# A windowed attention and highway kernel: four half-wide stages for the first pair of batches, other routes for V and for x, and one PSUM ring

## The chip, the cores and the metric

The kernel runs on one NeuronCore of a Trainium2 chip. The metric is device time in microseconds (us) of one execution; less is better. A core has a matrix engine (PE), a vector engine (DVE), an activation engine (ACT), a general engine (POOL) and a queue engine (SP). PE's weight loads stand beside it in the profile as PEld. Each engine runs its own instructions in order, and a wait at the head of an engine's list holds everything behind it.

## The reference

Eight batches (B), eight heads (H), 576 positions (S), head size 64 (D). Attention with a causal window of 128 positions and an ALiBi bias, then a highway layer on the 4608 x 512 result:

```python
mask = (rel >= 0) & (rel < 128)                    # rel = query position - key position
scores = where(mask, q @ k.T / 8 - slope[h] * rel, -1e9)
x = softmax(scores) @ v                            # (B, H, S, D) -> (B*S, H*D)
H_ = maximum(x @ w_h, 0)
T_ = sigmoid(x @ w_t + b_t)
out = T_ * H_ + (1 - T_) * x
```

Inputs and output are float32. Both kernels compute in bfloat16 with float32 sums.

## The kernel before, in words

Batches are taken in pairs; a pair is called a duo here (`m` = 0 to 3), and `r` is the batch within it. A duo has two stages (`s`), and a stage has eight units, one per head. The queries and keys of a sequence are cut into blocks of 128 rows, with a tail of 64 rows (`S` = 4 x 128 + 64).

For a duo the kernel does this:

- **Loads.** `load_qk`, `load_tails` and `load_v` issue DMAs from POOL that read float32 from HBM and write bfloat16 into SBUF (QL, KL, the tails QTL and KTL, and VA). All buffers are double, so a duo can be loaded while the one before it is computed. For duo 0 the first two heads of q and k are loaded ahead of the other six. A DMA issued from POOL occupies POOL while its descriptors are written, and it can also wait there until an earlier DMA has landed.
- **Transposes of q and k.** `transposes` writes two heads at a time through PE into one PSUM bank (`ps_tr`), and `evac` copies the bank to QT (DVE) or KT (ACT, for the first duo mostly DVE).
- **A unit.** `scores` (PE; four or eight matmuls into the single two-bank tile `sc`), `soft` (ACT: the exponential, 128 x 1024 elements, with the bias and the scale), `mask` (DVE: one multiplication by a table MK of window and decay), `pv` (PE: probabilities times V, with a column of ones that gives the row sum), `norm` (DVE: a reciprocal and a multiplication, from PSUM into x).
- **A block of the highway layer.** When all eight heads of a stage are normalized, each of its 4 or 5 blocks of 128 rows goes through `f_xt` (PE: four transposes of x), `f_xe` (ACT: copy to `xt`), `f_h` (PE: four matmuls of 512 columns), `f_u` (DVE: max(h,0) - x), `f_z` (PE: four matmuls of 512 columns, and a fifth that adds the bias), `f_th` (ACT: tanh), `f_t` (POOL), `f_g` (DVE), `f_out` (POOL) and `f_st` (SP: four stores of 32 rows, or two for a tail block).

The bias matmul of `f_z` has one row: `ones1` is 1 x 128 and `bT` is 1 x 512.

PSUM has eight banks: `RING = {"sc": 1, "tr": 2, "av": 2, "a": 1, "z": 1}`, where `sc` has two banks and each of the others one.

The order of the instructions on each engine is written out by a planner at the end of the function. It knows a cost for each piece (`node(...)`), its dependencies and a due time, advances a clock per engine, and emits the pieces in the order of their planned starts. The order that it finds is fixed; at run time each engine follows it and waits where something is late. The planner's DMA model is one queue with a rate; it knows nothing of the waits of a DMA for earlier ones.

Of the kernel before, what the change touches and what calls it, by code (L numbers as in the profile page):

```python
# [10 lines left out]
P = 128  # L11
# [3 lines left out]
def kernel(  # L15
# [10 lines left out]
    nc = tc.nc  # L26
# [14 lines left out]
    SLOT, LOOK = 2200, 100  # L41
    NBLK = (4, 5)
# [3 lines left out]
    p0p = ctx.enter_context(tc.tile_pool(name="p0", bufs=12))  # L46
    p1p = ctx.enter_context(tc.tile_pool(name="p1", bufs=5))
    smp = ctx.enter_context(tc.tile_pool(name="small", bufs=4))
    xp = ctx.enter_context(tc.tile_pool(name="x", bufs=3))
    fx = ctx.enter_context(tc.tile_pool(name="fx", bufs=3))  # L50
    op = ctx.enter_context(tc.tile_pool(name="ot", bufs=4))
    ft = ctx.enter_context(tc.tile_pool(name="ft", bufs=3))
    RING = {"sc": 1, "tr": 2, "av": 2, "a": 1, "z": 1}
    ps_sc, ps_tr, ps_av, ps_a, ps_z = (
        ctx.enter_context(tc.tile_pool(name="ps_" + n, bufs=b, space=PSUM))
        for n, b in RING.items()
    )
    RING.update({"p0": 12, "p1": 5, "x": 3, "xt": 3, "uu": 3, "tt": 3, "ot": 4})

# [10 lines left out]
    def load_qk(m, hs=slice(0, H), which=(0, 1)):  # L70
        i = m % 2
        for w in which:
            src, dst = ((q, QL), (k, KL))[w]
            if hs == slice(0, H):
                nc.gpsimd.dma_start(
                    out=dst[i][:].rearrange("p r h n -> p (r h) n"),
                    in_=src[2 * m : 2 * m + 2, :, 0:512, :].rearrange(
                        "r h (p t) d -> p (r h) (t d)", t=4
                    ),
                )  # L80
                continue
            for r in range(2):
                nc.gpsimd.dma_start(  # L83
                    out=dst[i][:, r, hs, :],
                    in_=src[2 * m + r, hs, 0:512, :].rearrange(
                        "h (p t) d -> p h (t d)", t=4
                    ),
                )

    def load_tails(m, which=(0, 1)):  # L90
        i = m % 2
        for w in which:
            src, dst = ((q, QTL), (k, KTL))[w]
            for r in range(2):
                nc.gpsimd.dma_start(
                    out=dst[i][:, :, r, :],
                    in_=src[2 * m + r, :, 512:S, :].rearrange("h s d -> s h d"),
                )

    def load_v(m, cs):  # L100
        i = m % 2
        for c in cs:
            n = min(P, S - c * P)
            nc.gpsimd.dma_start(  # L104
                out=VA[i][0:n, c, :, :, 0:D].rearrange("s r h d -> s (r h) d"),
                in_=v[2 * m : 2 * m + 2, :, c * P : c * P + n, :].rearrange(
                    "r h s d -> s (r h) d"
                ),
            )


# [48 lines left out]
    def c_vec():  # L160
        nc.vector.memset(ones1[:], 1.0)
        for h in range(H):
            nc.vector.memset(cvec[:, h : h + 1], float(np.exp(-float(P) * slopes[h])))
# [20 lines left out]
    def load_w(n):  # L184
        if n == 2:
            nc.gpsimd.dma_start(out=bT[:], in_=moe_b_t.rearrange("(o n) -> o n", o=1))
# [7 lines left out]
    TR = {}  # L194
    EV = {
        (m, w, hp): "ACT" if w and (m or hp == 0) else "DVE"
        for m in range(ND) for w in (0, 1) for hp in range(5)
    }

    def transposes(m, w, hp):  # L200

        i = m % 2
        pt = ps_tr.tile([P, 1024], BF16, name="pt")
        TR[m, w, hp] = pt
        if hp < 4:
            L = (QL, KL)[w][i]
            for hl in range(2):
                for t in range(4):
                    for r in range(2):
                        nc.tensor.transpose(  # L210
                            out=pt[r * D : (r + 1) * D,
                                   hl * 512 + t * P : hl * 512 + (t + 1) * P],
                            in_=L[:, r, 2 * hp + hl, t * D : (t + 1) * D],
                            identity=ident[:],
                        )
        else:
            L = (QTL, KTL)[w][i]
            for h in range(H):
# [4 lines left out]
                )  # L223

    def evac(m, w, hp):
        i = m % 2
        pt = TR.pop((m, w, hp))
        cp_ = nc.scalar.copy if EV[m, w, hp] == "ACT" else nc.vector.tensor_copy
        if hp < 4:
            if w == 0:  # L230
                nc.vector.tensor_copy(
                    out=QT[i][:, 2 * hp : 2 * hp + 2, 0:512],
                    in_=pt[:].rearrange("p (h n) -> p h n", h=2),
                )
            else:
                cp_(
# [371 lines left out]
```

## Time and profile before

| | |
|---|---|
| time of three runs | 212.14, 213.17 and 213.84 us, median 213.17 |
| the profiled execution | 213.98 us, of which the span is 212.3 |
| mean granted TensorE clock in the profile | 0.924 |
| busy: PE, DVE, ACT, POOL | 173.5, 142.4, 124.2, 119.5 us |
| bytes that DMA moved | 24.97 MB |

The page of the profile gives the busy time of each engine, then the span in 40 slices of 5.3 us (a digit is the busy share in tenths; PEclk is the clock that PE was granted, and DMA is the mean busy share of the 16 DMA engines), then groups of instructions by line and the chain of work that ended last. Other views show who waited for whom, the instructions in order of time, and the busy time in chosen stretches. A busy PE in these rows is not a PE at its peak: an instruction's record ends at a modelled time, and the records of neighbouring instructions overlap. The distance from the start of one group of matmuls to the start of the next is the better measure of what it occupies.

### The profile page before, as it was taken

To read this page: it belongs to the slowest core of one execution; us is meant where nothing else is said; L and a number is where in the kernel's file an instruction comes from. 1 tells how busy PE (TensorE), PEld (TensorE's weight loads), DVE (VectorE), ACT (ScalarE), POOL (GpSimd) and SP (SyncE) were. 2 spreads that over 40 slices of the span, in tenths; PEclk is the share of its full clock that TensorE was granted. 3 is DMA by queue.
4 is the path that set the end of the run, shared out by engine and by line. 5 is a ranking of instruction groups with operands and counts; after the bars stand their busy time and mean duration, and the time that the engine had idled before them with its cause. 6 is when DMAs were issued, how large, how long until landed. Compare 5 with 4: busy or idle time off the path is not lost.

```text
span 212.3 us, 5013 instructions
## 1 busy us (share of the span) xinstructions
PE 173.5 (82%) x2004; PEld 95.4 (45%) x2004; DVE 142.4 (67%) x308; ACT 124.2 (58%) x161; POOL 119.5 (56%) x137
## 2 busy tenths in 40 slices
PE   0547765995079679999999999999999999997940
PEld 0325443573045422556565445566453455543410
DVE  5626767570094164898886988897789979873550
ACT  2340355657023544889878868877878778824420
POOL 7993493429365395845333896543345564554662
PEclk9999999999555855999999999999999999999995
DMA  5599999999999999994223999322223333324244
GB/s 60 57 195 175 181 173 141 199 172 136 121 196 212 212 165 167 127 199 124 63 54 73 109 114 186 82 54 49 57 70 77 73 79 73 79 51 99 52 98 99
DMA packets 70135, 24.97 MB, mean 118 GB/s; under 512 B 48096, under 2 KB 65504, under 8 KB 70112
## 3 DMA queue, kind: packets, MB, share of 16 engines
q0 software_dynamic: 63328, 15.21, 90.9%
q1 hardware_dynamic: 6784, 9.45, 18.1%
q8 instruction: 15, 0.25, 0.5%
q14 instruction: 8, 0.07, 0.1%
HBM read 30.41 MB, written 9.44 MB: 188 GB/s over the span
## 4 chain that ended last, share of the span: by engine, by line
PE 57%; DMA 25%; POOL 10%; issue 2%; ACT 2%; DVE 1%; POOLq 1%; SPq 0%; ACTq 0%; DVEq 0%
DMA kl<-in_k_dram 19%; PE pz L381 14%; PE pa L364 13%; PE sc L274 8%; PE av L310 8%; DMA va<-in_v_dram 6%; PE pz L383 5%; PE pt L210 4%; PE pt L346 4%; POOL va L104 3%; POOL ql L83 2%; POOL kl L83 1%; POOL ot L403 1%; ACT pt L284 1%; POOL tri L142 1%
## 5 line engine op out<-in xcount | busy, mean ns | idle before, releaser
L284 ACT ACTIVATE pt<-sc,bias 128x1024 bf16<-128x1024 f32 x64 | 71.3, 1115 | 40.9 <-PE sc L274 40.7
L403 POOL TENSOR_TENSOR ot<-uu,x 128x512 f32<-128x512 bf16 x36 | 45.4, 1262 | 21.6 <-DVE uu L399 18.1
L295 DVE TENSOR_TENSOR pt<-pt,mk 128x1024 bf16<-128x1024 bf16 x64 | 49.1, 769 | 6.0 <-ACT pt L284 5.5
L394 POOL TENSOR_SCALAR tt<-tt 128x512 f16<-128x512 f16 x36 | 23.1, 641 | 37.6 <-ACT tt L390 34.7
L310 PE MATMUL av<-va,pt 128*128 128x65 bf16 (+1 forms) x576 | 33.2, 206 | 9.5 <-DVE pt L295 8.0
L364 PE MATMUL pa<-wH,xt 128*128 128x512 bf16 x144 | 39.6, 400 | 1.2 <-ACT xt L356 0.7
L381 PE MATMUL pz<-wT,xt 128*128 128x512 bf16 x144 | 39.8, 401 | 0.2 <-ACT tt L390 0.2
L310 PEld LDWEIGHTS <-pt 128*128 128x128 bf16 (+1 forms) x576 | 25.5, 105 | 23.4 <-DVE pt L295 8.9
L390 ACT ACTIVATE tt<-pz 128x512 f16<-128x512 f32 x36 | 21.6, 599 | 22.0 <-PE pz L383 20.4
L372 DVE SCALAR_TENSOR_TENSOR uu<-pa,x 128x512 bf16<-128x512 f32 x36 | 24.7, 686 | 14.1 <-PE pa L364 14.0
L274 PE MATMUL sc<-qt,kt 64*128 64x256 bf16 (+2 forms) x384 | 28.5, 258 | 5.1 <-ACT pt L284 3.4
L336 DVE TENSOR_TENSOR x<-av,rd 128x256 bf16<-128x256 f32 (+1 forms) x64 | 29.3, 458 | 2.2
L104 POOL DMA_DIRECT2D va<-in_v_dram x20 | 22.2, 1112 | 12.7 <-DMA kl<-in_k_dram 4.2
L399 DVE TENSOR_TENSOR uu<-uu,tt 128x512 bf16<-128x512 bf16 x36 | 16.1, 448 | 17.6 <-POOL tt L394 16.8
L356 ACT COPY xt<-pt 128x512 bf16<-128x512 bf16 x36 | 20.9, 583 | 6.3 <-PE pt L346 6.2
L335 DVE RECIPROCAL rd<-av 128x4 f32<-128x4 f32 (+1 forms) x64 | 11.7, 183 | 15.6 <-PE av L310 15.1
L274 PEld LDWEIGHTS <-kt 64*128 64x128 bf16 x384 | 13.7, 98 | 16.2 <-issue 11.5
L381 PEld LDWEIGHTS <-xt 128*128 128x128 bf16 x144 | 12.3, 101 | 14.4 <-issue 4.3
L346 PE MATMUL pt<-ident,x 128*128 128x128 bf16 x144 | 15.3, 231 | 3.7 <-DVE x L336 3.7
L364 PEld LDWEIGHTS <-xt 128*128 128x128 bf16 x144 | 12.3, 100 | 12.8 <-issue 3.6
L210 PE MATMUL pt<-ident,ql 128*64 128x128 bf16 x256 | 11.8, 244 | 6.9 <-POOL ident L127 5.0
L210 PE MATMUL pt<-ident,kl 128*64 128x128 bf16 x256 | 12.9, 256 | 3.9 <-DMA kl<-in_k_dram 2.2
(42 smaller groups left out, 123.1 us busy)
## 6 DMA issues: line engine op xcount, KB each, us to landing
out_dram<-ot SPq DMA_DIRECT2D x128, 64.0 KB, 1.7
va<-in_v_dram POOLq DMA_DIRECT2D x16, 256.0 KB, 9.3
ql<-in_q_dram POOLq DMA_DIRECT2D x3, 1024.0 KB, 15.6
kl<-in_k_dram POOLq DMA_DIRECT2D x3, 1024.0 KB, 18.1
out_dram<-ot SPq DMA_DIRECT2D x8, 128.0 KB, 2.3
ql<-in_q_dram POOLq DMA_DIRECT2D x2, 384.0 KB, 5.6
kl<-in_k_dram POOLq DMA_DIRECT2D x2, 384.0 KB, 7.9
qtl<-in_q_dram POOLq DMA_DIRECT2D x8, 64.0 KB, 16.5
```

Source lines behind the costliest of these rows:

```text
L104: nc.gpsimd.dma_start(out=VA[i][0:n, c, :, :, 0:D].rearrange("s r h d -> s (r h) d"), in_=v[2 * m : 2 * m + 2, :, c * P : c * P + n, :].re ...
L210: nc.tensor.transpose(out=pt[r * D : (r + 1) * D, hl * 512 + t * P : hl * 512 + (t + 1) * P], in_=L[:, r, 2 * hp + hl, t * D : (t + 1) * D ...
L274: nc.tensor.matmul(out=sc[:, r, off : off + w], lhsT=KT[i][rows, h, j * P : (j + 1) * P], rhs=rhs, start=True, stop=True,)
L284: nc.scalar.activation(out=pt[:], in_=SC.pop(u)[:], func=ACTF.Exp, bias=BIAS[:, h : h + 1], scale=scale,)
L295: nc.vector.tensor_tensor(out=o, in0=o, in1=mk, op=ALU.mult)
L310: nc.tensor.matmul(out=av[rows, g, :], lhsT=pt[:, r, off : off + w], rhs=va[:, j, r, h, :], start=n == 0, stop=n == len(terms) - 1,)
L336: nc.vector.tensor_tensor(out=x[:, 0:nb, h * D : (h + 1) * D], in0=av[:, 0:nb, 0:D], in1=rd[:, 0:nb].to_broadcast([P, nb, D]), op=ALU.mult,)
L346: nc.tensor.transpose(out=pt[:, c * P : (c + 1) * P], in_=X[st][:, b, c * P : (c + 1) * P], identity=ident[:],)
L364: nc.tensor.matmul(out=pa[:], lhsT=xt[:, c, :], rhs=wH[:, c, :], start=c == 0, stop=c == NCK - 1)
L372: nc.vector.scalar_tensor_tensor(out=uu[:], in0=pa[:], scalar=0.0, in1=X[st][:, b, :], op0=ALU.max, op1=ALU.subtract,)
L381: nc.tensor.matmul(out=pz[:], lhsT=xt[:, c, :], rhs=wT[:, c, :], start=c == 0, stop=False)
L403: nc.gpsimd.tensor_tensor(out=ot[:], in0=UU.pop((st, b))[:], in1=X[st][:, b, :], op=ALU.add)
```

## The change

- **Duo 0** is done in four stages `a` to `d` of half the width. Stage `a` gives query block 0, `b` block 1, `c` block 2, and `d` block 3 with the tail. Its q and k are loaded in two chunks of 64 partitions (256 positions, all heads and both batches), and the transposes of a chunk are 64 x 64. Between the two chunks POOL issues the weights. Duos 1 to 3 keep two stages, called `A` and `B`.
- **V** is loaded by DMAs from SP as float32 into a ring of two tiles (`vs`), and POOL casts each tile into VA.
- **PSUM** is one ring of four tiles of two banks each. A tile holds the scores of one unit (two in half-wide stages), the q and k transposes of one part, the results of `pv` for two heads, h and z of one block, or the transposes of one block of x.
- **mask and norm** work on two heads in one instruction.
- **x** of the stages from the fifth on (those of duos 1 to 3) is transposed by a DMA from SP straight into `xt`, which has five buffers; in duo 0 it still goes through PE and ACT.
- **The bias matmul** has all 128 rows: `ones1` and `bT` are zero but for row 0.
- **The planner** has new costs and due times. It models eight lanes for POOL's DMAs, the landing of SP's, and rings whose tiles are taken in turn; due times are shifted by constants per kind of piece.

The diff, cut to its core:

```diff
+    STAGES = {
+        "A": ((0, 0, 0), (0, 1, 128), (1, 1, 256), (1, 2, 384)),
+        "B": ((2, 2, 0), (2, 3, 128), (3, 3, 256), (3, 4, 384), (4, 4, 448)),
+        "a": ((0, 0, 0), (0, 1, 128)),
+        "b": ((1, 1, 0), (1, 2, 128)),
+        "c": ((2, 2, 0), (2, 3, 128)),
+        "d": ((3, 3, 0), (3, 4, 128), (4, 4, 192)),
+    }
+    ORDER = ("abcd", "AB", "AB", "AB")
+    DMA_X = tuple(range(4, 20))
+    BUFS = {
+        "ps": 4, "pA": 5, "pB": 3, "pf": 9, "vs": 2, "x": 3, "xt": 5, "uu": 3, "tt": 3, "ot": 3,
+    }
-    RING = {"sc": 1, "tr": 2, "av": 2, "a": 1, "z": 1}
+    def ps_tile(dt=F32):
+        return psp.tile([P, 2, 512 if dt == F32 else 1024], dt, name="ps")
...
+    def load_qk(m, w, x):
+        src, dst = ((q, QL), (k, KL))[w]
+        ps = slice(0, P) if x is None else slice(64 * x, 64 * x + 64)
+        nc.gpsimd.dma_start(out=dst[m % 2][ps].rearrange("p r h n -> p (r h) n"), ...
...
-            nc.gpsimd.dma_start(
-                out=VA[i][0:n, c, :, :, 0:D].rearrange("s r h d -> s (r h) d"),
+        nc.sync.dma_start(
+            out=vs[0:n],
+            in_=v[2 * m : 2 * m + 2, :, c * P : c * P + n, :].rearrange("r h s d -> s (r h) d"),
+        )
+    def cast_v(m, c):
+        nc.gpsimd.tensor_copy(
+            out=VA[m % 2][0:n, c, :, :, 0:D].rearrange("s r h d -> s (r h) d"),
+            in_=VS.pop((m, c))[0:n],
+        )
...
-    ones1 = cp.tile([1, P], BF16, name="ones1")
+    ones1 = cp.tile([P, P], BF16, name="ones1")
-    bT = cp.tile([1, DM], BF16, name="bT")
+    bT = cp.tile([P, DM], BF16, name="bT")
...
+    def mask(m, kind, g):
+        rep, lo, W = {"A": (4, 0, 256), "B": (2, 0, 512), "d": (2, 256, 256)}.get(kind, (2, 0, 256))
+        o = PT[m, kind, g][:].rearrange("p h r (j w) -> p h (r j) w", w=W)
+        mk = MK[:, 2 * g : 2 * g + 2, lo : lo + W].rearrange("p h (o w) -> p h o w", o=1)
+        nc.vector.tensor_tensor(out=o, in0=o, in1=mk.to_broadcast([P, 2, rep, W]), op=ALU.mult)
...
+        nc.vector.reciprocal(out=rd[:, :, 0:nb], in_=av[:, :, :, D : D + 1])
+        nc.vector.tensor_tensor(
+            out=x.rearrange("p b (h d) -> p h b d", h=2), in0=av[:, :, :, 0:D],
+            in1=rd[:, :, 0:nb].to_broadcast([P, 2, nb, D]), op=ALU.mult,
+        )
+    def f_xd(m, kind, b):
+        xt = fx.tile([P, NCK, P], BF16, name="xt")
+        XT[m, kind, b] = xt
+        nc.sync.dma_start_transpose(out=xt[:], in_=X[m, kind][:, b, :])
...
+                if stage_no in DMA_X:
+                    node(("x", kb), "SP", 700, t - 1.3 * dt, lambda kb=kb: f_xd(*kb), alln, take="xt", uses=[xo], land=1)
+                else:
+                    node(("xp", kb), "PE", 230, t - 1.0 * dt, lambda kb=kb: f_x(*kb), alln, take="ps", uses=[xo])
+                    node(("x", kb), "ACT", 590, t - 0.9 * dt, lambda kb=kb: f_xe(*kb), [("xp", kb)], take="xt", uses=[("xp", kb)])
```

In duo 0 the order of POOL's loads is: chunk 0 of q and of k, the two weight matrices and the bias, chunk 1 of q and of k, the tails. V's first block is loaded from SP at the start, and the others are spread over the duo.

More of the change, by code (lines that the diff above doesn't have):

```diff
@@ L336, in norm, with blocks @@
         nc.vector.tensor_tensor(
[L337 to L344 removed]
+            out=o, in0=o, in1=mk.to_broadcast([P, 2, rep, W]), op=ALU.mult,
+        )
+    def blocks(kind):
+        qs = [qb for j, qb, _ in STAGES[kind] if j == qb]
+        return [(r, qb) for r in range(2) for qb in qs if qb < 4] + [(None, 4)] * (4 in qs)
@@ L577 @@
+    SHIFT = {
[4 rows of a table added]
+    }
+    LOOKS = {"PE": 145, "ACT": 132, "DVE": 0, "POOL": 1001, "SP": 0}
+    order, end = plan(SHIFT, LOOKS)
     with tc.manual_schedule():
```

693 lines of the change are left out of this document (359 added, 334 removed), and 4 rows, old and new, of the table SHIFT.

## The prediction

> **What bounds the kernel now.** The page comes first, for where in the span PE is full and where it is not.
>
> ```profile
> PE   0547765995079679999999999999999999997940
> ...
> PEclk9999999999555855999999999999999999999995
> ```
>
> A slice is 5.3 us. From slice 17 (some 85 us) to slice 36 (some 190 us) PE is full. Before that it has holes, and in slices 11 to 16 a clock near half speed. So each stretch has its own limit. The view by windows gives the numbers; its columns are PE, PEld, DVE, ACT, POOL busy, clock, DMA share and GB/s.
>
> ```profile
> 50.00:86.50 36.50, 24.81 (x209) 12.13 (x205) 15.47 (x32) 14.49 (x18) 22.88 (x26) 0.63 2.28 173
> 114.07:152.33 38.26, 38.26 (x504) 21.07 (x505) 32.60 (x71) 30.90 (x40) 21.93 (x24) 1.00 0.75 95
> ```
>
> The timeline of PE shows one turn of the rhythm; the columns are start and length in us, then the instruction.
>
> ```profile
> 110.23 1.04 PE L381 MATMUL pz<-wT,xt 128*128 128x512 bf16 x4
> 111.20 0.39 PE L383 MATMUL pz<-bT,ones 1*128 1x512 bf16 x1
> 111.52 0.60 PE L310 MATMUL av<-va,pt 128*128 128x65 bf16 x12
> 112.05 0.40 PE L274 MATMUL sc<-qt,kt 64*128 64x256 bf16 x8
> 112.38 0.40 PE L346 MATMUL pt<-ident,x 128*128 128x128 bf16 x4
> 112.62 1.03 PE L364 MATMUL pa<-wH,xt 128*128 128x512 bf16 x4
> 113.48 0.59 PE L310 MATMUL av<-va,pt 128*128 128x65 bf16 x12
> 114.01 0.39 PE L274 MATMUL sc<-qt,kt 64*128 64x256 bf16 x4
> ```
>
> ```profile
> 152.26 0.39 PE L274 MATMUL sc<-qt,kt 64*128 64x256 bf16 x4
> ```
>
> Scores in a group of four are a duo's first stage, in a group of eight its second. So 114.01 is the first score of duo 2 and 152.26 that of duo 3: 38.26 us apart (the window runs from the one to the other, 0.06 later), and PE is busy in all of it. A steady duo costs what PE needs; DVE with 32.6 is next. I write the end of the span as t1 + 3P + L: P is a duo's period, L what is left after the last period, t1 the start of duo 1 as the steady rhythm would have it. Here P = 38.26, t1 = 114.07 - 38.26 = 75.8, and L = 212.3 - 152.33 - 38.26 = 21.7. Of the 75.8, one duo's work is 38.3; the start costs 37.5 us beside its work. The timeline says where a good part of that goes.
>
> ```profile
> 56.74 0.68 POOL L95 DMA_DIRECT2D ktl<-in_k_dram  x1 [2.08 <-DMA va<-in_v_dram]
> 57.45 0.63 POOL L394 TENSOR_SCALAR tt<-tt 128x512 f16<-128x512 f16 x1
> 58.12 0.42 DVE L399 TENSOR_TENSOR uu<-uu,tt 128x512 bf16<-128x512 bf16 x1 [11.36 <-POOL tt L394]
> ...
> 80.01 1.89 PE L364 MATMUL pa<-wH,xt 128*128 128x512 bf16 x4
> ```
>
> POOL's list holds the loads of a later duo ahead of `f_t`, and these wait for V loads to land. `f_t` runs at 57.45, and DVE has stood 11.36 us at `f_g` with masks and norms behind it. The price is paid twice: long after the hole h's four matmuls still take 1.89 us, and 1.03 in the row at 112.62. The rest of the 37.5 us is the wait for first data:
>
> ```profile
> 10.09 0.61 PE L274 MATMUL sc<-qt,kt 64*128 64x256 bf16 x4 [1.10 <-ACT kt L236]
> ...
> 37.94 1.89 PE L364 MATMUL pa<-wH,xt 128*128 128x512 bf16 x4
> ```
>
> The first scores come at 10.1, the first highway block at 37.9, since all eight heads of a full stage must be through.
>
> **The steady duo (P).** From start to start in the rows of one turn, x's transposes occupy 112.62 - 112.38 = 0.24 us, h's four matmuls 113.48 - 112.62 = 0.86, z's five 111.52 - 110.23 = 1.29. Five plain matmuls of 0.215 are 1.08, so the bias matmul of one row costs 0.21 more than one of 128 rows should. Nine blocks give 9 x 0.24 = 2.2 and 9 x 0.21 = 1.9. All other PE work of duos 1 to 3 keeps its instructions, so PE's floor is 38.26 - 4.1 = **34.2**. If the extra 0.21 is not due to the one row, it is 36.1.
>
> DVE, in the same window:
>
> ```profile
> L295 DVE TENSOR_TENSOR pt<-pt,mk 128x1024 bf16<-128x1024 bf16 x16 | 12.2, 760 | 0.2 <-ACT pt L284 0.2
> L336 DVE TENSOR_TENSOR x<-av,rd 128x320 bf16<-128x320 f32 (+1 forms) x16 | 7.3, 458 | 0.6
> L372 DVE SCALAR_TENSOR_TENSOR uu<-pa,x 128x512 bf16<-128x512 f32 x9 | 6.2, 686 | 0.8 <-PE pa L364 0.6
> L399 DVE TENSOR_TENSOR uu<-uu,tt 128x512 bf16<-128x512 bf16 x9 | 3.8, 419 | 0.3 <-POOL tt L394 0.2
> L335 DVE RECIPROCAL rd<-av 128x5 f32<-128x5 f32 (+1 forms) x16 | 2.9, 184 | 2.3 <-PE av L310 2.2
> L231 DVE COPY qt<-pt 128x1024 bf16<-128x1024 bf16 x4 | 2.8, 690 | 1.0 <-PE pt L210 1.0
> ```
>
> ```profile
> L336 DVE TENSOR_TENSOR x<-av,rd x64: 423/458/493, 24.9 to 191.2; 128x256 bf16<-128x256 f32 x32, 128x320 bf16<-128x320 f32 x32
> L295 DVE TENSOR_TENSOR pt<-pt,mk x64: 679/686/1544, 12.0 to 187.2; 128x1024 bf16<-128x1024 bf16 x64
> ```
>
> From 256 to 320 columns a norm grows from 423 to 493 ns, 1.1 ns a column, so 0.14 us of it is fixed. Eight pairs save 8 x (0.14 + 0.18), with one reciprocal less: 2.6 us. For a mask of double size the ends are 1.37 (two medians) and 1.23 (the same fixed part saved): 0 to 1.1 us a duo; I take 1.0, near the norm. DVE falls from 32.6 to 29. Its cover against a bound is 5 us; what may eat it is POOL.
>
> ```profile
> L403 POOL TENSOR_TENSOR ot<-uu,x 128x512 f32<-128x512 bf16 x10 | 12.1, 1206 | 5.1 <-DVE uu L399 4.2 <-DMA out_dram<-ot 0.9
> L104 POOL DMA_DIRECT2D va<-in_v_dram x5 | 5.6, 1129 | 0.1
> L394 POOL TENSOR_SCALAR tt<-tt 128x512 f16<-128x512 f16 x9 | 5.6, 622 | 11.7 <-ACT tt L390 10.5 <-DMA out_dram<-ot 1.2
> ```
>
> POOL trades five descriptor writings of 1.13 for five casts of 1024 columns, which no row shows. One input costs 0.62 for 512 columns, so 1.24 from below; two inputs and a float32 side cost 1.21, so 2.4 from above. POOL's 21.9 becomes 22.5 to 28.3; I take the lower end, a cast having one input. But a POOL instruction can hold DVE: masks have a median of 0.69 and a longest of 1.54, which would be a wait of 0.85. Five casts cost DVE between nothing and 5 x 1.24 = 6.2, and at that end DVE needs 35 and is the bound. I take 1, like the mean mask of 0.760 in place of 0.686. The Trainium skill, in SBUF — State Buffer, Who interferes with whom, says that a DVE instruction with two SBUF inputs contends with a GpSimd instruction that reads SBUF. The spread of the masks agrees with it.
>
> ACT loses nine copies; its 30.9 was not the bound.
>
> ```profile
> L284 ACT ACTIVATE pt<-sc,bias 128x1024 bf16<-128x1024 f32 x16 | 17.9, 1116 | 5.3 <-PE sc L274 5.3
> L356 ACT COPY xt<-pt 128x512 bf16<-128x512 bf16 x10 | 5.8, 585 | 0.0
> L390 ACT ACTIVATE tt<-pz 128x512 f16<-128x512 f32 x9 | 5.4, 602 | 2.1 <-PE pz L383 2.1
> ```
>
> SP gets the transposes and V's loads.
>
> ```profile
> L419 SPq DMA_DIRECT2D out_dram<-ot x128: 314/422/1403, 61.9 to 207.9; - x128
> ...
> DMA to landing us min/median/max: 1.6/1.7/6.4
> ```
>
> Stores occupy SP for (8 x 4 + 2) x 0.42 = 14.3 us a duo, V adds 5 x 0.42 = 2.1. No row shows a DMA transpose. From below it issues like a store, 0.42; from above it holds SP until it has landed, as the slowest store did, 6.4. I take 0.8, near the store, since SP's rows are issue alone, and a landing of 2 to 3 us, which five `xt` buffers hide. SP then has 14.3 + 2.1 + 7.2 = 24 of 34. What stands behind a transpose on SP are stores, and behind these POOL's `f_out` with three `ot` buffers.
>
> The last term is the ring. A duo takes 16 tiles for scores, 8 for `pv`, 9 for blocks and 5 for q and k: 38 in 34.2 us, 0.9 apart, so that of four tiles each may be held 3.6 us. A block's tile lives from the first h to the end of tanh, 0.86 + 1.08 + 0.60 and two handovers, some 2.8, and 3.9 where an exponential of 1.1 stands ahead on ACT. So some waits at tiles will show on PE: between nothing and all that was gained. I take 1.8, a little under half: **P = 36.0**, between 34.2 and 38.3.
>
> **The start (t1).** POOL has no V loads left, so `f_t` can wait only behind q and k. In the window from 50 us DMA moves 173 GB/s of bfloat16, which is 350 of float32. Chunk 0 of q and k (2.1 MB) and V's first block (0.5 MB) then take 7 us, with 2 to issue and land: transposes near 9, stage `a` near 12. The weights (2.1 MB) and chunk 1 (2.1 MB) follow at some 15 and 22. Near 22 stage `a` is through, and its two highway blocks run while chunk 1 is turned. From there DVE is the fuller engine. Up to t1 it owes evacuations (q 6 x 0.69, k three times double that, tails 0.8: 9), masks (16 of half size, 11), norms (10, as before) and u and g of three or four blocks (4): 34 us. At the 85% to which DVE is full in the steady window that is 40, from 10 on: **t1 = 50**, and I take 51 for cold matmuls. PE's 128 extra transposes of 64 x 64 cost at most 0.06 each by the row at 112.38, 7.7 us; with DVE behind, they are covered, without that cover they would be late in full. From below the loads bind: 9.2 MB of duo 0 and duo 1's q and k, 4.2, are 38 us, and with landing, transposes and evacuation 46. From above, with DVE 60% full, 66.
>
> **The end (L).** After the last norm a transpose by DMA (2 to 3 us) takes the place of PE and ACT (0.24 + 0.59 and handovers), and five blocks are 0.45 us shorter: 21.7 + 1.8 - 2.2, about **21.5**; 20 to 24.
>
> **Sum.** 51 + 3 x 36.0 + 21.5 = 180.5 of span. The profiled execution took 213.98 with a span of 212.3, 1.7 more, and lay 0.8 over the median of the runs shown: 180.5 + 1.7 - 0.8 = **181.4 us**.
>
> **The rivals.**
>
> PE's gain turns into other waits (tiles, masks behind casts): P stays 38.3, and 51 + 115 + 21.5 + 0.9 = 188. For it: DVE was at 85%. Against: DVE gets lighter.
>
> The first duo stays slow, with DVE 60% full among small instructions and matmuls on half clock: t1 = 65, and 65 + 108 + 21.5 + 0.9 = 195. For it: the 1.89 at 37.94, where PE was not dense. Against: data come by rows for all heads, and the highway starts some 15 us sooner.
>
> The stall doesn't go, and the change fails to do what it says: a cast waits for its V load in POOL's order, q and k loads for earlier ones, and `f_t` behind both. t1 stays 75.8: 206. Against: of eleven loads a duo on POOL six are left.
>
> DMA transposes are the bound, and the kernel gets slower. If each takes c in single file, on SP or beyond it, SP's duo is 16.4 + 9c, and it decides from c = (36 - 16.4) / 9 = 2.2 us on. At c = 3.4 P is 47 and the end 51 + 141 + 21.5 + 0.9 = 214.4; nine landings one after the other at 5.2, within the stores' 1.6 to 6.4, give the same. Against: stores overlap, four of 0.42 issued within one landing of 1.7. The Trainium skill speaks for this rival: VectorE: DVE Perf Modes, The three transpose paths, has a 128 x 128 transpose at 390 ns on TensorE and 1309 ns by DMA, and four of the latter in a row are 5.2 us a block, an estimate. The trace disagrees on the first figure: four of them occupy TensorE for 0.24 us here.
>
> **How the numbers follow.** The forecast (t1 46 to 60, P 34.2 to 37.5) gets 0.58, the rivals in their order 0.15, 0.13, 0.08 and 0.06. The range runs from 46 + 3 x 34.4 + 20.5 + 0.9 = 171 to 66 + 3 x 36.5 + 22.5 + 0.9 = 199, which leaves out the last two rivals and the corners. Only these two could end within 1% (2 us, about what a measurement of this kernel can tell from no change) or beyond: faster 0.92, same 0.03, slower 0.05.
>
> **What would show it.** DVE's wait of 11.36 us is gone, and no half clock lies after 50 us. The first highway block is near 22, duo 1's first score near 51, and those of duos 2 and 3 are 36 us apart. z's five matmuls take 1.08. PE has short waits for ACT or DVE at new tiles. I am wrong if SP is full with h waiting for DMA, or if DVE is under 70% in the first 50 us.

## The result, and the profile after

The changed kernel takes 219.28 us (median of four runs, 218.74 to 221.67), the kernel before 212.74 beside it: a ratio of 1.032, 95% interval 1.023 to 1.041. It is slower, where 181.4 was forecast. The span of its profiled execution is 217.5 us, 5.2 more than before's.

The page of the changed kernel, in slices of 5.4 us:

```profile
PE   0057997491797975758989899939989799988330
...
PEclk9999999999998899996999999976999999999885
```

PE's plateau of nines is gone. The long stretch of half clock is shorter too (a clock of 0.50 is left from 144 to 150 us), so the mean clock rose from 0.924 to 0.949, and yet the time is longer. The timeline of PE gives the first scores of duos 1, 2 and 3:

```profile
68.21 0.39 PE L292 MATMUL ps<-qt,kt 64*128 64x256 bf16 x4
108.35 0.39 PE L292 MATMUL ps<-qt,kt 64*128 64x256 bf16 x4
149.78 0.61 PE L292 MATMUL ps<-qt,kt 64*128 64x256 bf16 x4
```

P is 40.1 and 41.4 us where before had 38.26 and the forecast 36.0, and t1 is 68.2 where 51 was forecast. First scores can be planned early, so for comparisons I use the last norm of each duo, from the timeline of DVE: first the kernel before, then the changed one.

```profile
74.94 0.49 DVE L336 TENSOR_TENSOR x<-av,rd 128x320 bf16<-128x320 f32 x1
118.25 0.49 DVE L336 TENSOR_TENSOR x<-av,rd 128x320 bf16<-128x320 f32 x1
156.48 0.49 DVE L336 TENSOR_TENSOR x<-av,rd 128x320 bf16<-128x320 f32 x1
191.18 0.49 DVE L336 TENSOR_TENSOR x<-av,rd 128x320 bf16<-128x320 f32 x1
```

```profile
78.14 0.56 DVE L357 TENSOR_TENSOR x<-ps,rd 128x384 bf16<-128x384 f32 x1
118.10 0.82 DVE L357 TENSOR_TENSOR x<-ps,rd 128x640 bf16<-128x640 f32 x1
157.78 0.82 DVE L357 TENSOR_TENSOR x<-ps,rd 128x640 bf16<-128x640 f32 x1
187.41 0.82 DVE L357 TENSOR_TENSOR x<-ps,rd 128x640 bf16<-128x640 f32 x1
```

The first duo, for which the change does most, ends 3.2 us later than before. Duo 1 makes that up, duo 2 takes 39.7 in place of 38.2, and duo 3, which has no next duo to turn, 29.6 in place of 34.7. From the last norm to the end of the span it is 30.1 us in place of 21.1, with eight highway blocks still without their tanh where before had five. So attention ends 3.8 us sooner and the kernel 5.2 later. In the window between the last norms of duos 1 and 2 (columns as in the prediction) PE is busy for 34 of 40 us, and DVE for 31:

```profile
118.10:157.78 39.68, 34.15 (x451) 19.74 (x456) 31.30 (x47) 25.25 (x30) 23.17 (x23) 0.91 0.59 129
```

The 11.4 us stall of DVE did not go; it became two. The first is the weights: they stand in POOL's list behind the first duo's two chunks and also behind duo 1's q and k, the first highway block waits for them (PE), and DVE stands 6.40 us at the block's `f_u`, which waits for z in the same tile. The second has the old shape with a new cause: POOL stands at casts until V lands, and `f_t` and then DVE's `f_g` stand behind it. V's loads wait themselves, too: there are two fp32 tiles, and a load on SP waits until a cast on POOL has freed one, 38.4 us in eight waits (the last line, from the waits of SP).

```profile
39.64 0.58 PE L387 MATMUL ps<-wH,xt 128*128 128x512 bf16 x1 [1.91 <-DMA wH<-in_moe_w_h_dram]
...
44.91 0.69 DVE L393 SCALAR_TENSOR_TENSOR uu<-ps,x 128x512 bf16<-128x512 f32 x1 [6.40 <-PE ps L403]
...
50.85 1.04 POOL L119 CAST va<-vs 128x1024 bf16<-128x1024 f32 x1 [2.23 <-DMA vs<-in_v_dram]
52.94 1.04 POOL L119 CAST va<-vs 128x1024 bf16<-128x1024 f32 x1 [1.05 <-DMA vs<-in_v_dram]
53.96 0.61 POOL L412 TENSOR_SCALAR tt<-tt 128x512 f16<-128x512 f16 x1
...
54.60 0.43 DVE L417 TENSOR_TENSOR uu<-uu,tt 128x512 bf16<-128x512 bf16 x1 [7.88 <-POOL tt L412]
...
SPq L110 <- POOL va L119: 38.4, 8, 15.0
```

At the end a transpose of x stands in SP's list behind twelve stores, and h waits for it:

```profile
195.82 6.53 SPq L436 DMA_DIRECT2D out_dram<-ot  x12
202.45 1.20 SPq L365 DMA_TRANSPOSE xt<-x  x1
203.75 9.76 SPq L436 DMA_DIRECT2D out_dram<-ot  x20
...
204.91 1.46 PE L387 MATMUL ps<-wH,xt 128*128 128x512 bf16 x4 [4.41 <-DMA xt<-x]
```

The waits of the engines name one more suspect. ACT's tanh waits for DVE's `f_u`, 34 times: h and z share a tile, u waits for z's last matmul, and tanh, another reader of the tile, waits for u.

```profile
ACT tt L408 <- DVE uu L393: 60.6, 34, 6.1
```

### The profile page after: what moved, and what is told of

Read it like the earlier page. It is cut to its first block, busy times and chain, and to the rows that moved or that the text cites. A ratio compares the mean times of both kernels' runs of the same rounds, so it can differ in the third digit from the quotient of the medians.

```text
span 217.5 us, 5032 instructions
## 1 busy us (share of the span) xinstructions
PE 157.8 (73%) x2001; PEld 92.8 (43%) x2024; DVE 144.1 (66%) x238; ACT 109.8 (50%) x150; POOL 120.2 (55%) x133
## 4 chain that ended last, share of the span: by engine, by line
DMA 26%; PE 23%; DVE 14%; POOL 11%; issue 10%; ACT 6%; SPq 6%; POOLq 1%; ACTq 0%; DVEq 0%
DMA ql<-in_q_dram 10%; DMA vs<-in_v_dram 9%; PE ps L387 8%; PE ps L401 7%; SPq L436 6%; DMA out_dram<-ot 5%; DVE uu L393 4%; DVE pt L317 4%; POOL tt L412 4%; ACT tt L408 3%; DVE uu L417 3%; POOL ot L422 3%; PE ps L340 3%; POOL va L119 2%; ACT pt L307 2%
## 5 line engine op out<-in xcount | busy, mean ns | idle before, releaser
L307 ACT ACTIVATE pt<-ps,bias 128x1024 bf16<-128x1024 f32 (+1 forms) x80 | 71.3, 951 | 3.8 <-PE ps L292 3.8
L408 ACT ACTIVATE tt<-ps 128x512 f16<-128x512 f32 x36 | 21.5, 597 | 60.8 <-DVE uu L393 60.6
L387 PE MATMUL ps<-wH,xt 128*128 128x512 bf16 x122 | 39.7, 413 | 16.3 <-DMA xt<-x 5.1
L412 POOL TENSOR_SCALAR tt<-tt 128x512 f16<-128x512 f16 x36 | 30.6, 850 | 32.6 <-ACT tt L408 29.6
L317 DVE TENSOR_TENSOR pt<-pt,mk 128x2048 bf16<-128x2048 bf16 (+1 forms) x40 | 47.7, 1198 | 1.1 <-ACT pt L307 1.0
L393 DVE SCALAR_TENSOR_TENSOR uu<-ps,x 128x512 bf16<-128x512 f32 x36 | 24.8, 688 | 29.9 <-PE ps L403 25.4
L401 PE MATMUL ps<-wT,xt 128*128 128x512 bf16 x143 | 40.1, 404 | 1.3 <-DMA wT<-in_moe_w_t_dram 1.1
L292 PE MATMUL ps<-qt,kt 64*128 64x256 bf16 (+2 forms) x384 | 27.8, 258 | 10.0 <-DVE x L357 5.8
L119 POOL CAST va<-vs 128x1024 bf16<-128x1024 f32 (+1 forms) x20 | 21.0, 1050 | 19.0 <-DMA vs<-in_v_dram 14.7
L340 PE MATMUL ps<-va,pt 128*128 128x65 bf16 (+1 forms) x576 | 25.9, 200 | 7.2 <-ACT tt L408 2.9
L340 PEld LDWEIGHTS <-pt 128*128 128x128 bf16 (+1 forms) x576 | 21.1, 103 | 14.7 <-issue 5.8
L357 DVE TENSOR_TENSOR x<-ps,rd 128x256 bf16<-128x256 f32 (+3 forms) x40 | 25.5, 638 | 1.4
L292 PEld LDWEIGHTS <-kt 64*128 64x128 bf16 x384 | 13.8, 98 | 23.0 <-issue 12.8
```

The costliest lines, as they stand in the source:

```text
L292: nc.tensor.matmul(out=sc[:, r, o + off : o + off + w_], lhsT=KT[i][rows, h, j * P : (j + 1) * P], rhs=rhs, start=True, stop=True,)
L307: nc.scalar.activation(out=PT[m, kind, h // 2][:, h % 2], in_=SC[m, kind, h][:, :, o : o + W], func=ACTF.Exp, bias=BIAS[:, h : h + 1], sca ...
L317: nc.vector.tensor_tensor(out=o, in0=o, in1=mk.to_broadcast([P, 2, rep, W]), op=ALU.mult,)
L340: nc.tensor.matmul(out=av[rows, hl, n * (D + 1) : (n + 1) * (D + 1)], lhsT=pt[:, hl, r, off : off + (D if narrow else P)], rhs=va[:, j, r, ...
L387: nc.tensor.matmul(out=az[:, 0, :], lhsT=XT[m, kind, b][:, c, :], rhs=wH[:, c, :], start=c == 0, stop=c == NCK - 1)
L393: nc.vector.scalar_tensor_tensor(out=uu[:], in0=AZ[m, kind, b][:, 0, :], scalar=0.0, in1=X[m, kind][:, b, :], op0=ALU.max, op1=ALU.subtract,)
```

## The experiments

Every edit of a dependency, a cost or a ring lets the planner write the whole order anew, so a kernel differs from its neighbour by the edit and what the planner makes of it.

**Four suspects, each by itself.** The first edit gives h and z tiles of their own:

```diff
-        "ps": 4,
+        "ps": 3, "a": 1, "z": 1,
 ...
-        az = ps_tile()
+        az = psa.tile([P, 512], F32, name="pa")      # and one for z from a pool of its own
```

> The changed kernel with h and z of a highway block in tiles of their own (one bank each), the ring then three tiles of two banks; the dispatch order is planned anew from the same costs. Theory 1 (one tile for h and z makes u wait for z's last matmul and tanh for u, and ACT, standing at tanh, holds the exps and the ring): u no longer waits for L403, tanh no longer for u, the PE waits for tanh at tiles go, the distance of the duos falls from 40 to 41 us to 37 to 38, and the time from 219.3 to 209 to 213 us. Theory 3 (the shared ring of few big tiles is itself what holds PE): with three tiles in place of four the waits grow, the distance is 41 to 43 us, the time 220 to 226. Theory 2 (the loss is x by DMA, above all at the end): 218 to 220.

It took 220.8 us, ratio to before 1.039 (1.031 to 1.048). Tanh no longer waits for u but for z's last matmul (47.9 us in 32 waits), and the later duos are faster: from duo 0's last norm to duo 3's 102.8 us in place of 109.3. But duo 0's came at 84.7 in place of 78.1. So the later duos went as theory 1 had it, and the first as theory 3 would have it; but in the first duo the trace shows PE standing 5.64 us for weights and DVE 6.75 us for `f_t`, and that the ring of three is the cause there is not shown. The sum is nothing.

```diff
-    DMA_X = tuple(range(4, 20))
+    DMA_X = ()                                        # and "xp": 0 among the shifts
```

> The changed kernel with x transposed by TensorE in all stages and copied out by ACT, as in the first four, the four transposes planned at the block's own place (shift 0 for them). Theory 2 (x by DMA costs more than it saves: landing 2.5 us behind stores in SP's order, 4.4 us of PE's wait near 205 us): the wait in the tail goes, the time falls by 4 to 6 us to 213 to 215. Theory 1 and 3 (the tile for h and z, the ring): a further ring tile for each block, 27 copies of 0.6 us on ACT, 0.24 us of PE for each block: 0 to 6 us slower, 219 to 225, with the distance of the duos 41 to 43.

224.9 us, 1.059 (1.052 to 1.066): 5.6 us above the changed kernel, as theories 1 and 3 had it. The end did get shorter, 26.0 us after the last norm, and the three duos after the first got longer, by 8.6 in all.

```diff
-        "th": -8.55, ..., "vl": 6.43, "x": 7.93,
+        "th": -8.55, ..., "vl": 6.43, "w": -14.25, "x": 7.93,
```

> The changed kernel with the weights' loads moved ahead together with q's and k's (the same shift for them), so that wH and wT are issued ahead of duo 1's q and k. Theory 5 (the first duo is late because its highway blocks wait for weights that stand behind duo 1's loads): the first highway block comes near 24 to 28 us in place of 39.6, duo 1's first score from 68.2 to 60 to 63, the time falls by 4 to 7 us to 212 to 215. Theory 4 (DVE stands because POOL stands at V's casts ahead of f_t, whatever the weights): the wait of 7.9 us at the gate's product stays near 50 to 55 us, duo 1 starts at 66 to 68, the time is 217 to 220.

226.7 us, 1.065 (1.056 to 1.074). Both theories' times were missed, and theory 5 failed: the first highway block came at 47.6 us, not at 24 to 28. The shift put the weights ahead of chunk 1 as well, and POOL's tail loads, now behind duo 1's q and k, held POOL for 7.8 and 7.4 us with casts behind them.

The bias by itself, in the kernel before:

```diff
-    ones1 = cp.tile([1, P], BF16, name="ones1")
-    bT = cp.tile([1, DM], BF16, name="bT")
+    ones1 = cp.tile([P, P], BF16, name="ones1")       # zero but for row 0
+    bT = cp.tile([P, DM], BF16, name="bT")
```

> The kernel before with the bias' matmul over 128 rows (zeros but for the first row, in weights and bias) and nothing else. The step of the sum as it stands in the prediction takes 0.21 us for each block; the changed kernel's trace shows five matmuls of z in 1.17 us where they took 1.29, 0.12 us, so 1.1 us for each duo. If PE's time is what sets the distance of the duos: 3 to 5 us off the time, 208 to 210, the distance 37.1. Rival 1 of the prediction (what PE gains turns into other waits): the distance stays 38.3, the time 212 to 213.

206.48 us (six runs), 0.973 (0.966 to 0.979): this part alone gains some 6 us (by the ratio 5.8, interval 4.4 to 7.2), more than the 3 to 5 expected. PE's timeline shows z's five matmuls in 121.02 - 119.93 = 1.09 us, where they took 1.29:

```profile
119.93 1.04 PE L383 MATMUL pz<-wT,xt 128*128 128x512 bf16 x4
120.80 0.38 PE L385 MATMUL pz<-bT,ones 128*128 128x512 bf16 x1
121.02 0.34 PE L312 MATMUL av<-va,pt 128*128 128x65 bf16 x6
...
112.18:149.09 36.91, 36.91 (x505) 21.59 (x502) 32.82 (x71) 30.79 (x40) 21.77 (x24) 1.00 0.79 98
```

From duo 2's first score to duo 3's, the last row above, it is 36.91 in place of 38.26, and PE is full in all of it: where PE is the bound, most of what PE saves is saved (1.35 us of 0.20 x 9 = 1.8 a duo). The reverse edit in the changed kernel (one row again):

> The changed kernel with the bias' matmul over one row again (the same instructions, two operands cut to one row), nothing else. In the kernel before this one edit was worth 6 to 7 us. If PE's time still sets the distance of the duos in the changed kernel: 5 to 7 us slower, 224 to 226. If waits set it (PE is busy 35 of 41 us there): 0 to 2 us slower, 219 to 221.

220.45 us, 1.039 (1.032 to 1.046), 1.2 above the changed kernel, whose own interval overlaps with it. The edit adds less PE time there, since scores of 64 rows follow and not `pv`: 1.27 us for z's five in place of 1.17 or 1.18, some 0.09 x 36 = 3.2 in all. At most a part of that reaches the time; PE is not the bound.

**x by DMA in the kernel before** (with the bias, 206.5), for the five stages of duos 1, 2 and half of 3:

```diff
+    DMA_X = (2, 3, 4, 5, 6)
+                if st in DMA_X:
+                    node(("xe", kb), "SP", 700, t - 1.3 * dt, lambda kb=kb: f_xd(*kb), alln, land=1)
```

> The kernel before with the bias over 128 rows (206.5 us by itself) and, in the stages of duos 1 and 2 and the first of duo 3, x transposed by a DMA on SP in place of four TensorE transposes and an ACT copy; five tiles for it in place of three; the rest as before. The prediction's step: 0.24 us of PE for each block, 2.2 for each of the two duos whose every block it takes, about 5 for 22 blocks: 201 to 203. Rival (transposes by DMA land late behind SP's stores, the PE waits for xt, as in the second kernel's tail with 4.4 us): 206 to 210, with waits of PE for x by DMA in the table of groups.

218.3 us, 1.036 (1.029 to 1.043): a loss of 12 us where I expected a gain of 4. SP's timeline has the transposes behind twelve stores, which themselves wait for `f_out`; h waits 5.50 us, and the clock in the window is 0.72:

```profile
110.35 8.28 SPq L427 DMA_DIRECT2D out_dram<-ot  x12
118.79 7.27 SPq L366 DMA_TRANSPOSE xt<-x  x5
...
126.47 1.49 PE L372 MATMUL pa<-wH,xt 128*128 128x512 bf16 x3 [5.50 <-DMA xt<-x]
...
116.00:134.00 18.00, 11.24 (x115) 5.57 (x114) 9.11 (x21) 8.16 (x10) 9.15 (x9) 0.72 1.73 121
```

The same transposes issued by ACT, with no store ahead of them:

> The kernel before with the bias over 128 rows and x by DMA in the same 22 blocks as in the run before (218.3 us), but with the DMA transposes issued by ACT in place of SP, so that no store stands ahead of them. Theory 2a (what x by DMA cost there, 12 us, is SP's order: transposes behind up to 12 stores, 5.5 us of PE's wait and half clock after it): the waits of PE for xt by DMA fall to under 3 us in all, the clock is above 0.92, the time 202 to 208. Rival (the transposes themselves, landing 2.5 us or up to 10, or ACT's time for the issues, 1.2 us where the copy took 0.58): 210 to 218.

212.7 us, 1.007 (1.002 to 1.011), inside the rival's range: without SP's order 5.6 of the 12 are gone. What is left agrees with late landings, in the timeline of PE and in the summary of the tile, but ACT's time for 22 issues (some 1.2 us each, where a copy takes 0.58) was not told apart from them:

```profile
122.70 1.89 PE L372 MATMUL pa<-wH,xt 128*128 128x512 bf16 x4 [3.69 <-DMA xt<-x]
...
DMA to landing us min/median/max: 2.4/3.2/8.5
```

While the next duo's V is loaded the transposes land late, h waits 3.69 us, and the granted clock goes from 1.00 (118 to 122 us) to 0.62 (122 to 124). In the changed kernel the last stage alone by TensorE:

> The changed kernel with x of the last stage alone transposed by TensorE and copied by ACT; the stages before it by DMA as they were. Theory 2 for the tail (PE waits 4.4 us near 205 us for a transpose that stands behind 12 stores): from the last norm to the end 26 to 27 us in place of 30.1, the time 214.5 to 216.5. Rival (the tail is set by the stores, 20 of them after 203.7 us, and by the number of highway blocks left at the last norm): 218 to 221.

216.0 us, 1.023 (1.014 to 1.031). From the last norm to the end it is 26.1 us in place of 30.1, as theory 2 said of the tail.

**V and the loads.** Duo 1's q and k after duo 0's casts:

```diff
-                            [("tr", m - 2, w, p_) for p_ in (...)]))
+                            [("tr", m - 2, w, p_) for p_ in (...)]
+                            + [("v", 0, c) for c in range(5)] * (m == 1)))
```

> The changed kernel with duo 1's q and k loads issued after the five casts of duo 0's V (a dependency in the planner alone; no other load is moved by hand). Theory 6 (the first 42 us are the DMA engines' at 95 to 99 per cent and some 185 GB/s, and duo 1's 2 MB stand ahead of the weights, the tails and their waits on POOL, 22 us of POOL's standing there by 45 us): the first highway block comes near 28 to 32 us in place of 39.6, duo 0's last norm at 68 to 72 in place of 78.1, the time is 211 to 215. Rival (duo 1's loads are then what comes too late, the engine time of the DMAs is the same to the end of duo 0): duo 0's last norm 70 to 74, but duo 1's last norm stays near 118 and the time 218 to 221.

221.4 us, 1.049 (1.041 to 1.058). Neither came as written: duo 0's third stage ended at 53.9 us, ten sooner than in the changed kernel, and its last at 83.1, five later, with POOL standing 10.0, 6.4 and 3.8 us at casts for V. Then the casts on ACT (`nc.scalar.copy`, else the changed kernel):

> The changed kernel with V's 20 casts on ACT in place of POOL, the loads unchanged. Theory 4 (POOL's casts hold f_t and the masks: 7.9 us of DVE's wait at the gate's product near 54.6, masks of up to 3.8 us beside casts): the masks' mean goes from 1.20 to 1.15 us or less, f_t's and the product's waits shrink, duo 0's last norm comes 3 to 6 us earlier, the time is 213 to 217. Rival (the cast waits for its V load wherever it stands, and ACT, which gives out the exps in order, now stands there): 220 to 228.

224.3 us, 1.066 (1.056 to 1.075): the rival. ACT now stands where POOL stood:

```profile
ACT va L119 <- DMA vs<-in_v_dram: 37.1, 8, 10.0
```

V as before, by casting DMAs from POOL, with duo 1's q and k after it:

```diff
-        vs = vsp.tile([P, 2 * H, D], F32, name="vs")
-        nc.sync.dma_start(out=vs[0:n], ...)
+        nc.gpsimd.dma_start(out=VA[m % 2][0:n, c, :, :, 0:D].rearrange(...), ...)
```

> The changed kernel with V loaded as before by casting DMAs on POOL, without fp32 tiles and casts, and duo 1's q and k after duo 0's V (which alone gave 221.4 us, with POOL standing 10.0, 6.4 and 3.8 us at casts for V's loads). Theory 4a (POOL stands at the casts until V lands, and f_t and the gate's product behind it): DVE's waits for f_t of 11.6 us go, duo 0's last norm comes at 66 to 74 in place of 83, the time is 208 to 215. Rival (the DMA engines are what is late, and V comes no sooner): duo 0's last norm 78 to 83, the time 217 to 222.

212.3 us, 1.001 (0.996 to 1.006), 9 under the one without this edit. Duo 0's last norm came at 60.5 us, 23 sooner. But duo 1's came 55 us later: POOL had issued the first of duo 1's V ahead of its q and k. (The 7.2 us for q that the expectation of a later run names is PE's wait for first data at the start of the run.) What holds duo 1 is POOL standing at the rest of V's loads until q and k have landed, with `f_t` behind them, DVE behind `f_t`, and PE at the transposes of duo 1's q:

```profile
67.73 1.20 POOL L108 DMA_DIRECT2D va<-in_v_dram  x1 [4.48 <-DMA ql<-in_q_dram]
72.70 1.15 POOL L108 DMA_DIRECT2D va<-in_v_dram  x1 [3.77 <-DMA kl<-in_k_dram]
...
74.53 1.37 DVE L415 TENSOR_TENSOR uu<-uu,tt 128x512 bf16<-128x512 bf16 x1 [10.82 <-POOL tt L410]
...
77.24 1.92 PE L239 MATMUL ps<-ident,ql 128*64 128x128 bf16 x32 [9.00 <-ACT tt L406]
```

The reverse, V by SP and casts in the kernel before (with the bias, and five fp32 tiles):

> The kernel before with the bias over 128 rows (206.5 us) and V by fp32 loads on SP and casts on POOL, with five fp32 tiles. Theory 4a (casts hold POOL until V lands): duo 0's and 1's stages get later, 209 to 216 us, with POOL waiting over 10 us for V's loads. Rival (fewer DMAs on POOL's own queue, V issued early on another one: the load was the first duo's limit): duo 0's last norm from 75.6 to 68 to 72, 200 to 205 us. Neither: 205 to 208.

225.6 us, 1.067 (1.061 to 1.073), 19 above 206.5, as theory 4a has it, but by another way: POOL waited only 7.7 us for V. SP's list held fifteen of V's loads from 0.8 to 89.7 us, each waiting for a free tile, and the first store behind them. POOL's `f_out` then waits for an `ot` buffer and, behind it, DVE and h. The timelines of POOL and PE:

```profile
99.90 1.15 POOL L416 TENSOR_TENSOR ot<-uu,x 128x512 f32<-128x512 bf16 x1 [12.24 <-DMA out_dram<-ot]
...
104.10 1.86 PE L377 MATMUL pa<-wH,xt 128*128 128x512 bf16 x4 [9.63 <-DVE uu L385]
```

So V's loads on SP's list hold the stores as well. Parts taken together:

> The changed kernel with h and z in tiles of their own (ring of three), x of the last stage by TensorE, V by casting DMAs on POOL and duo 1's q and k after it. From the single runs: the stages from duo 0's last norm to the last norm took 102.8 us in place of 109.3 with the tiles apart, the tail 26.1 in place of 30.1. If the parts add up and duo 0's last norm comes by 74: 203 to 209. If the ring of three holds up the first duo as it did alone (duo 0's last norm at 84.7): 212 to 218.

215.7 us, 1.018 (1.011 to 1.025): the parts do not add up. Duo 0's last norm came at 64.9, duo 1's at 125.8.

**The order of the loads.** V on POOL, duo 1's q and k after three chunks of duo 0's V, duo 1's V after its q and k, the last stage's x by TensorE:

> The changed kernel with V by casting DMAs on POOL, duo 1's q and k after the first three chunks of duo 0's V, duo 1's V after its q and k, and x of the last stage by TensorE. Theory 6a (with V on POOL the first duo can end at 60 us and what made duo 1 late in the run before, 7.2 us for q and 9.0 behind it with POOL issuing duo 1's V ahead of its q and k, is the order of the loads): duo 1's last norm comes near 104 to 108 us in place of 115.7, the time is 200 to 206. Rival (the DMA engines are full to 100 us whatever the order, 97 to 99 per cent): duo 1's last norm 112 to 118, the time 207 to 212.

**199.55 us, 0.940 (0.934 to 0.946)**, faster than both kernels. Duo 0's to duo 3's last norms:

```profile
69.95 0.56 DVE L355 TENSOR_TENSOR x<-ps,rd 128x384 bf16<-128x384 f32 x1
107.26 0.82 DVE L355 TENSOR_TENSOR x<-ps,rd 128x640 bf16<-128x640 f32 x1
141.61 0.82 DVE L355 TENSOR_TENSOR x<-ps,rd 128x640 bf16<-128x640 f32 x1
171.25 0.83 DVE L355 TENSOR_TENSOR x<-ps,rd 128x640 bf16<-128x640 f32 x1
```

Then this kernel with V's way alone put back as the change has it:

> The kernel of 199.6 us with V by fp32 loads on SP and casts on POOL as in the changed kernel (two fp32 tiles), and the rest as there: duo 1's q and k after three of duo 0's chunks, last stage's x by TensorE. Theory 4a (V's way is the cause of most of the loss): 213 to 219 us, duo 0's last norm at 76 to 84, the stages from duo 1's last norm to duo 3's in 68 to 69 us in place of 64. Rival (the order of the loads and the tail made the gain): 200 to 206.

221.2 us, 1.046 (1.035 to 1.057): theory 4a, and 2 us more than its range (from duo 1's last norm to duo 3's it is 67.3). V's way costs 21.6 us here, in the spans 216.7 - 197.4 = 19.3. By the last norms (83.79, 123.33, 161.03, 190.65) 13.8 of that are lost in duo 0, 2.2 in duo 1, 3.4 in duo 2, none after that. The waits of POOL and of DVE:

```profile
POOL va L119 <- DMA vs<-in_v_dram: 37.0, 9, 7.0
...
DVE uu L417 <- POOL tt L412: 31.9, 14, 8.2
```

DVE's wait for `f_t` was 11.4 us with V on POOL, so it grew by 20.5, about what the span grew by. In the other pair with V's way alone between its runs, the two with duo 1's q and k late, it is 9.1 us (221.4 against 212.3); the changed kernel with only V's way put back was not run. And x by TensorE in all stages of the 199.6 kernel, its four transposes planned at the block's own place:

> The kernel of 199.6 us (V by POOL's DMAs, loads in order, last stage's x by TensorE) with x by TensorE and an ACT copy in all stages, planned at the block's own place. If the DMA transposes spare PE and the ring what the prediction's step said (0.24 us of PE and 0.59 of ACT for each of 22 blocks): 4 to 8 us slower, 203 to 208. If they cost more than they spare, as in the kernel before (6 us from ACT's queue, 12 from SP's): 192 to 199.

213.6 us, 1.012 (0.998 to 1.026), 14 us slower than with DMA, more than the first expectation. The distances of the last norms are 41.0, 40.4 and 33.1 in place of 37.3, 34.4 and 29.6. So x by DMA pays here and cost 6 to 12 us in the kernel before. One difference is seen: PE's waits for `xt` are 1.4 us in all in the 199.6 kernel, though a transpose lands late there too (median 3.9 us, longest 9.5), where they were 7.3 and 4.6 in the two kernels before with x by DMA. Eight blocks are open at the last norm here and not five, but that holds with TensorE in all stages too. Whether the ring tile saved, ACT's copy or the place of the transposes makes up the 14 us was not told apart. At last the tile of h and z, once nothing else stalls:

> The kernel of the run before with h and z in tiles of their own and a ring of three. Theory 1 (the shared tile serialises u and tanh): the distance of the stages from duo 1's last norm to duo 3's, 65 us in the run with V on POOL, falls by 3 to 5 us, the time is 3 to 5 us under the run before. Theory 3 (a ring of three is too few): the first two duos' stages get later by 3 to 7 us, the time is the same as the run before or up to 5 us above it.

204.3 us, 0.961 (0.956 to 0.966), 4.7 above the 199.6. Duo 0's last norm is as early (69.7), duo 1's 7 us later. PE stands there at h for a transpose that lands late:

```profile
97.01 1.49 PE L388 MATMUL pa<-wH,xt 128*128 128x512 bf16 x3 [6.60 <-DMA xt<-x]
```

Theory 1 fell: from duo 1's last norm to duo 3's it is 65.1 us in place of 64.0, though tanh waits 45.3 us for u in the kernel of 199.6. The time is the one that theory 3 gave, but the 7 us are that late transpose, so that a ring of three is too few is not shown.

## Why the prediction was wrong

**The step that failed first is "POOL has no V loads left, so f_t can wait only behind q and k".** V's loads left POOL, but their waits did not: a cast in POOL's order waits for its own load to land, which the issue of a casting DMA did not. That was the third rival, given 0.08 and priced for one place, the first duo (206). V's way alone is 19 us of span in the pair above, 5.6 of it in duos 1 and 2. The step that costed the casts asked how long one lasts (1.24 forecast, 1.05 measured) and what it does to masks; it never asked for what it waits. In that pair POOL stands 37.0 us at casts and DVE 31.9 us for `f_t`; in the changed kernel itself POOL stands 14.7 us at casts, in seven waits.

**t1: 68.2 in place of 51.** With V on POOL and the loads in order duo 1's first score comes at 57.55, 6.6 over the forecast. So the sum for the half-wide stages was nearer than 68.2 looks, but short even there. What the step did not do is read the order of POOL's issues. Text and sum let the weights follow chunk 0, ahead of chunk 1; POOL issues both chunks and all of duo 1's q and k ahead of them, since the planner's shift for q and k (-14.25) has no like for the weights:

```profile
5.90 1.18 POOL L89 DMA_DIRECT2D kl<-in_k_dram  x1
...
7.71 0.82 POOL L202 DMA_DIRECT2D wH<-in_moe_w_h_dram  x1
...
0.00:50.00 50.00, 29.87 (x464) 20.14 (x465) 26.12 (x59) 20.93 (x40) 20.74 (x34) 1.00 1.28 175
```

"The first highway block is near 22" was 39.6. The last line has DVE busy for 26.1 of the first 50 us, 52%, so the sign "DVE under 70%" came. The second rival (DVE 60% full, t1 = 65, chance 0.13) is nearest in size, but by luck: not small instructions hold DVE there, but the two waits of 6.40 and 7.88 us.

**P: 40.1 and 41.4 in place of 36.0.** By last norms 40.0 and 39.7; in the kernel of 199.6 they are 37.3 and 34.4. By first scores, as the prediction has it, the kernel of 199.6 has 37.5 and 38.6, so that 36.0 is not shown to be right without V's new way either: it is the first rival's 38.3 that comes near. The error was to let the old P, 38.3, be the upper end: an old bound at PE does not limit a new wait elsewhere. The bias gave 1.35 a duo where 1.9 was counted. The price of the ring (1.8, from a tile's life of 2.8) was argued wrongly: u and tanh follow one another, so that tiles live longer. The runs did not size that term. In these terms the kernel of 199.6 is 57.55 + 3 x 38.07 + 25.7 = 197.4 of span, 16.9 over the forecast's 180.5 (6.6 at the start, 6.2 in the duos, 4.2 at the end): V's way is the largest miss, and the forecast would have been 17 us of span short without it.

**L: about 26.9 in place of 21.5** (217.5 - 68.2 less three times 40.8, the mean of the two distances). I put the DMA transposes at the end at no more than the path they replace, and five blocks. Eight blocks were open instead, and the last stage's transposes, behind stores on SP, cost 4.0 us of it. Issue was sized at 0.8 us and is 1.2 (median 1.216); landing at 2 to 3 and is 2.5 in the median, but 5.2 at most here and 10.4 in the kernel before with x by DMA.

**What held.** PE's floor of 34.2 was not undercut by a full duo (34.4 at the least). Five matmuls in 1.08: 1.09 in the kernel before with the bias alone, 1.17 to 1.18 in the changed kernel. A double mask at 1.23 (1.22 undisturbed), so the step of the pairs was right, yet DVE's busy time stayed (142.4 to 144.1), since `f_g` went from 448 ns to 686 in the mean; without casts, in the kernel of 199.6, DVE is busy for 135.5. The fourth rival (transposes in single file) is not what happened: the transposes issue 1.2 us apart and land in 2.5 in the median, and what delays them on SP is what stands ahead.

What stays open: why V's loads land late, whether for the two fp32 tiles, for their place in SP's list or for full DMA engines (in the kernel of 221.2 stores and transposes behind V's loads cost little: POOL waits only 1.7 us for stores, and PE has no large wait for a transpose); and why x by DMA gains 14 us in one kernel and loses in the other.

## What to carry to other kernels

When a load with a cast inside is split into a plain load and a cast on an engine, the engine inherits the load's wait, and everything behind it in that engine's order waits too: cost the instruction by what it waits for, not by how long it lasts. For a DMA that is moved to another queue, write down what stands ahead of it there (here stores that wait for a last product), and for loads at the start write down the order of issue. A saving on an engine is worth its full size only while that engine is the bound; the bias gave some 6 us of 7.2 on PE in one kernel, and at most some 1 of 3.2 in the other.

## What the runs showed of the hardware

- A DMA transpose of a 128 x 512 block holds the issuing queue for 1.2 us (median of 27) and lands 2.4 us after issue at the least, 2.5 in the median of the changed kernel, and up to 10.4 in the kernel before with x by DMA, while the next duo's V is loaded.
- Work on POOL can hold a DVE instruction with two SBUF inputs. A mask of 1.22 us took 3.82, 2.6 more, beside the end of an `f_out` and two casts, where POOL is busy for 2.7 us:

```profile
78.22 1.17 POOL L422 TENSOR_TENSOR ot<-uu,x 128x512 f32<-128x512 bf16 x1
...
78.61 3.82 DVE L317 TENSOR_TENSOR pt<-pt,mk 128x2048 bf16<-128x2048 bf16 x1
...
79.33 2.02 POOL L119 CAST va<-vs 128x1024 bf16<-128x1024 f32 x2
```

  The Trainium skill, SBUF — State Buffer, Who interferes with whom, has such a product contend with GpSimd's reads; the trace agrees, and the size is the 2.6 us above. I had allowed 1 us a duo for it; DVE's busy time is 144.1 - 135.5 = 8.6 us above the kernel without casts, some 2.2 a duo.

- The bias matmul's cost depends on its neighbours. With one row z's four took 0.97 us and the bias 0.32; with 128 rows 0.87 and 0.22, where `pv` of 128 rows follows. In the changed kernel scores of 64 rows follow, and the bias takes 0.31 again. So each change of the number of rows seems to cost some 0.1 us; only these rows bear on it.
- Two engines that read one PSUM tile went one after the other, tanh behind `f_u` 34 times. h and z lie in different banks of the tile. The Trainium skill, PSUM — Partial Sum Buffer, PSUM bank collisions raise a hardware error, has a dependency added between instructions on different engines that touch the same bank; by that rule these two need none. With a tile for each, tanh waits for z's last matmul instead (47.9 us, 32 times), so here the order comes with the program's tile.
- POOL's DMA issues wait for older DMAs of its queue to land: 5.7 and 6.3 us at two tail loads near 28 and 36 us of the changed kernel, 4.5 and 3.8 at V's loads in the rows of POOL at 67.73 and 72.70 above. A load put early therefore also holds the computations that POOL has behind later loads.
